# Block-sparse attention with a softplus feed-forward: the products with V of a set's two units at one place

## The chip, the cores and the metric

The kernel runs on one core of one Trainium2 chip. The metric is the device time of one execution in microseconds (us), lower is better. Three runs of the kernel before took 807.98, 808.40 and 809.11 us; their median is 808.4 us.

## The reference

Attention over 4 batches and 8 heads, 768 positions, head size 64. Positions form 24 blocks of 32. A query block sees its own block and the two neighbours, the first and the last block, and three sampled blocks; the first and the last query block see everything. The result is the input of a feed-forward layer with a softplus between two matrix products.

```python
scores = scale * np.matmul(q, k.transpose(0, 1, 3, 2))
mask = np.abs(blk_i - blk_j) <= window
mask = mask | (blk_i == 0) | (blk_j == 0) | (blk_i == n_blocks - 1) | (blk_j == n_blocks - 1)
...
scores = np.where(mask, scores, -1000000000.0)
scores = scores - np.max(scores, axis=-1, keepdims=True)
attn = np.exp(scores)
attn = attn / (np.sum(attn, axis=-1, keepdims=True) + 1e-09)
out = np.matmul(attn, v)
x = out.transpose(0, 2, 1, 3).reshape(B * S, H * D)      # 3072 x 512
h = x @ w_in                                             # 3072 x 2048
g = np.maximum(h, 0.0) + np.log1p(np.exp(-np.abs(h)))
return g @ w_out                                         # 3072 x 512
```

All is computed in fp32: the attention with fp32 matmuls, the feed-forward with operands that are split into a high and a low part (three matmuls for one).

## The kernel before

**Sets and units.** Queries are taken in groups of four query blocks (128 rows), six groups to a batch. Each group is a *set*, numbered in order; the sixth group of a batch has only two query blocks left (a half set) and is preceded by a *whole* set, which holds the rows of the first and last query block that see all keys. That makes 28 sets: per batch five full ones, one whole, one half. A set works on four pairs of heads and is cut into two *units*: `a = 0` is the first two pairs of heads, `a = 1` the other two (`NA` is 2). So there are 56 units, `units[n] = (m, a)`.

**What a unit does**, in this order:

- `scores` (L581): the products of queries and gathered keys into two PSUM tiles (tag `s`; matmuls of L601, of L625 in a whole set), then on VectorE the scaling, the mask and the row minimum `nmax` (L607, or L632 and L638).
- `exponents` (L642): ScalarE's exponential of four pieces, L657, with row sums.
- `transposes` (L661): eight TensorE transposes (L670, twelve in a whole unit) into two or three PSUM tiles of tag `s`, each copied to an SBUF tile `pt` (four buffers) by ScalarE (L677) or VectorE (L675). In a unit `a = 1` that isn't whole both copies are ScalarE's.
- `values` (L682): the products of `pt` with the gathered V, `vg`, into the PSUM tile `x` (L700, 64 profiled matmuls in a unit of a full set, 32 in a half set; L714 in a whole set). The tile `x` has one buffer; it is made at the unit `a = 0` and holds both units.

When a set's second unit is done, `normalise` (L721, VectorE, L728 to L730) divides by the sums and frees `x`, `turn` (L738) transposes the result on TensorE (L745), `x_high` (L757, ScalarE, L759) and `x_low` (L761, VectorE, L763) split it for the feed-forward.

**Pieces.** `pieces(n)` (L768) gives three pieces for place `n`: the score piece (`x_low` of a set that ended two places ago, `scores(n + 2)`), the value piece (`exponents(n + 2)`, `turn` of a set that ended one place ago, `values(n)`, and behind a set's second unit `load_values` of the set after next into the same one of two `vg` buffers), and the transpose piece (`x_high`, `normalise` of a set that ends here, `transposes(n + 1)`). `attend` (L862) runs the next piece, one gather of V and of keys (GpSimd, L567 and L511), and a tick of the conversion of the feed-forward's weights (`convert`).

**Order.** The first 22 pieces run by themselves (L885). After that the pieces are strewn into the feed-forward's first phase by `due` (L888): one step `j` of the feed-forward is `hidden(j)` (12 matmuls, L237 to L239, a piece may stand in the middle), and `project(j - 3)` (9 matmuls, L295 to L297, a piece may stand after each third of it). In the steady stretch a step takes one unit: the score piece in the middle of `hidden`, the value piece after the first third of `project`, the transpose piece behind `project`. The second phase of the feed-forward has no pieces. SyncE's queue runs in the program's order; on the other engines a planner places the instructions, by the program's order where they are ready in its own reckoning. The four PSUM buffers of tag `s` are shared by `scores`, `transposes`, `turn` and `hidden`, so each of those waits for an earlier one to be read out.

Of the kernel before, what the change touches and what calls it, by code (L numbers as in the profile page):

```python
# [50 lines left out]
def sparse_attention_ffn(  # L51
# [27 lines left out]
    NA = NP // 2  # L79
# [385 lines left out]
    def gathered(work, m):  # L465
        while work and work[0][0] <= m:
            work.pop(0)[1]()
# [50 lines left out]
    sets = []  # L518
# [58 lines left out]
    units = [(m, a) for m in range(len(sets)) for a in range(NA)]  # L577
# [103 lines left out]

    def values(n):  # L682
        m, a = units[n]
        b, g, whole = sets[m]
        pt = state[n]["pt"]
        gathered(value_work, m)
        vd = vg[sets[m]]
        if a == 0:
            xps[m] = ps_x.tile([P, DM], F32, tag="x", name=f"x{n}")
        xq = xps[m]  # L690

        if not whole:
            ni = NI if g < NG - 1 else 2
            for j in range(2):
                for r in range(2):
                    h = 2 * (2 * a + j) + r
                    for c in range(2):
                        for i in range(ni):
                            rows = slice(i * BLOCK, (i + 1) * BLOCK)
                            nc.tensor.matmul(  # L700
                                xq[rows, h * D : (h + 1) * D],
                                pt[r, 2 * j + c][:, rows],
                                vd[:, c, i, h * D : (h + 1) * D],
                                start=(c == 0), stop=(c == 1),
                            )
        else:
            rows_v = vd.rearrange("p c i f -> p (c i) f")
            for r in range(2):
                at = (2 * a + r) * D
                for c in range(NCH):  # L710
                    for o in range(2):
                        rows = slice(64 * o, 64 * o + 64)
                        h = 2 * (2 * a + o) + r
                        nc.tensor.matmul(  # L714
                            xq[rows, at : at + D],
                            pt[r, c][:, rows],
                            rows_v[:, c, h * D : (h + 1) * D],
                            start=(c == 0), stop=(c == NCH - 1),
                        )
# [48 lines left out]
    def pieces(n):  # L768
# [24 lines left out]
        def value_piece():  # L793
            if n + 2 < len(units):
                exponents(n + 2)
            if ended[1] is not None:
                turn(ended[1])
            if n < len(units):
                values(n)
                if ended[2] is not None:  # L800
                    load_values(ended[2] + 2)
            if scored is not None:
                load_queries(scored + 2)
# [177 lines left out]
```

## Time and profile before

| | us |
|---|---|
| median of the runs | 808.4 |
| span of the profiled execution | 812.1 |
| TensorE matmuls busy (PE) | 781.7 |
| VectorE busy (DVE) | 574.8 |
| ScalarE busy (ACT) | 489.6 |
| GpSimd busy (POOL) | 223.3 |

The span is that of one execution under the profiler, from the first to the last instruction; it is 3.7 us longer than the median of the runs. Busy time is the union of an engine's instructions. Matmuls are pipelined and their ends are modelled, so a busy PE isn't PE at its peak. PEld is the loading of matmul weights, which overlaps PE. In rows of the profile a name such as `x<-vg,pt` is the tile written and the tiles read, and `[3.19 <-ACT pt L677]` is idle time of the engine ahead of the instruction with what ended it; "issue" is idle time in which the engine waited for nothing that the profile shows.

### The profile page before, as it was taken

How to read it: one execution, taken by the hardware profiler on the slowest of the kernel's cores; microseconds unless marked ns; L12 is line 12 of the kernel's file. 1: busy time of each engine (PE TensorE's matmuls, PEld its weight loads, DVE VectorE, ACT ScalarE, POOL GpSimd, SP SyncE). 2: the span in 40 equal slices, each digit the busy share in tenths (PEclk: the TensorE clock that was granted, in tenths of full speed). 3: DMA queues.
4: the chain of work that ended last, by engine and by line, in shares of the span. 5: the costliest groups of instructions: out<-in, count | busy, mean ns of one | idle time of the engine just before them, and what ended most of it. 6: DMA issues, size and time to landing. Idle time of an engine off the chain costs nothing.

```text
span 812.1 us, 21433 instructions
## 1 busy us (share of the span) xinstructions
PE 781.7 (96%) x8108; PEld 647.6 (80%) x8108; DVE 574.8 (71%) x1474; ACT 489.6 (60%) x1182; POOL 223.3 (27%) x389
## 2 busy tenths in 40 slices
PE   8878898999999999999999999999999999999997
PEld 8545676877677777778778988999988999988996
DVE  5778999876887777886655985656565656656564
ACT  5878785757767767767565764444444444444442
POOL 6864775635565436563000000000000000000000
PEclk9999898999999999999999999999999999999999
DMA  8899678687696777866425640304040312122021
GB/s 254 241 257 336 171 212 266 195 294 247 184 291 198 248 261 200 267 171 184 158 78 182 250 178 20 137 1 155 2 146 10 116 40 105 52 88 68 0 79 40
DMA packets 48408, 129.65 MB, mean 160 GB/s; under 512 B 5489, under 2 KB 5617, under 8 KB 46257
## 3 DMA queue, kind: packets, MB, share of 16 engines
q1 hardware_dynamic: 42304, 109.79, 42.3%
q0 software_dynamic: 5712, 17.57, 7.6%
q8 instruction: 64, 1.05, 0.5%
q10 hardware_dynamic: 288, 0.93, 0.3%
q14 instruction: 40, 0.32, 0.1%
HBM read 97.85 MB, written 30.41 MB: 158 GB/s over the span
## 4 chain that ended last, share of the span: by engine, by line
PE 82%; DVE 7%; ACT 6%; DMA 2%; issue 2%; POOL 0%; SPq 0%; ACTq 0%; DVEq 0%; POOLq 0%
PE o L295 11%; PE h L237 11%; PE o L297 10%; PE o L296 10%; PE h L238 10%; PE h L239 10%; PE s L601 5%; PE t L670 4%; PE x L700 4%; ACT pr L657 3%; PE warm L831 2%; DMA kT<-in_k_dram 1%; PE s L625 1%; DVE pr L607 1%; PE x L714 1%
## 5 line engine op out<-in xcount | busy, mean ns | idle before, releaser
L237 PE MATMUL h<-x,w 128*128 128x384 f32 x512 | 180.0, 352 | 0.4 <-DVE nmax L632 0.2
L238 PE MATMUL h<-x,w 128*128 128x384 f32 x512 | 173.7, 339 | 0.0
L239 PE MATMUL h<-x,w 128*128 128x384 f32 x512 | 173.1, 338 | 0.0
L250 DVE TENSOR_SCALAR u<-e 128x384 f32<-128x384 f32 x128 | 50.8, 397 | 155.8 <-ACT e L244 154.4
L295 PE MATMUL o<-w,gh 128*128 128x512 f32 x384 | 158.7, 413 | 0.0
L657 ACT ACTIVATE pr<-pr,nmax 128x256 f32<-128x256 f32 (+2 forms) x208 | 110.4, 532 | 74.6 <-DVE nmax L607 60.4
L297 PE MATMUL o<-w,gl 128*128 128x512 f32 x384 | 152.0, 396 | 1.2 <-issue 1.0
L296 PE MATMUL o<-w,gh 128*128 128x512 f32 x384 | 151.7, 395 | 0.0
L243 ACT ACTIVATE e<-h 128x384 f32<-128x384 f32 x128 | 62.4, 487 | 114.9 <-PE h L239 114.8
L267 ACT CAST gh<-u 128x384 fp32r<-128x384 f32 x128 | 65.6, 513 | 79.2 <-PE o L296 78.1
L237 PEld LDWEIGHTS h<-x,w 128*128 128x128 f32 x512 | 96.6, 189 | 19.4 <-issue 11.2
L567 POOL DMA_INDIRECT vg<-in_v_dram,ix x88 | 90.3, 1027 | 65.9 <-PE x L700 39.1
L238 PEld LDWEIGHTS h<-x,w 128*128 128x128 f32 x512 | 96.8, 189 | 6.5 <-issue 2.2
L511 POOL COPY kg<-kT 128x128 f32 x252 | 86.0, 389 | 41.2 <-PE s L601 38.8
L239 PEld LDWEIGHTS h<-x,w 128*128 128x128 f32 x512 | 96.6, 189 | 0.0
L295 PEld LDWEIGHTS o<-w,gh 128*128 128x128 f32 x384 | 72.0, 188 | 19.9 <-issue 7.1
L297 PEld LDWEIGHTS o<-w,gl 128*128 128x128 f32 x384 | 72.1, 188 | 18.8 <-issue 1.5
L296 PEld LDWEIGHTS o<-w,gh 128*128 128x128 f32 x384 | 72.2, 188 | 10.3 <-issue 0.4
L607 DVE CUSTOM_DVE_ANT_1 pr<-s,mask 128x256 f32<-128x256 f32 (+1 forms) x192 | 69.6, 414 | 14.5 <-PE s L601 14.5
L258 ACT ACTIVATE u<-u 128x384 f32<-128x384 f32 x128 | 66.9, 523 | 15.4 <-DVE e L252 15.2
L263 DVE TENSOR_TENSOR u<-u,e 128x384 f32<-128x384 f32 x128 | 73.6, 575 | 3.0 <-ACT u L258 2.4
L273 DVE TENSOR_TENSOR gl<-u,gh 128x384 fp32r<-128x384 f32 x128 | 73.0, 570 | 2.8 <-ACT gh L267 2.8
(81 smaller groups left out, 1088.6 us busy)
## 6 DMA issues: line engine op xcount, KB each, us to landing
vg<-in_v_dram SPq DMA_DIRECT2D x19, 768.0 KB, 5.8
xD<-x SPq DMA_DIRECT2D x8, 1536.0 KB, 7.4
x<-xD SPq DMA_DIRECT2D x8, 1536.0 KB
raw<-in_w_in_dram SPq DMA_DIRECT2D x16, 512.0 KB, 9.3
raw<-in_w_out_dram SPq DMA_DIRECT2D x16, 512.0 KB, 8.3
qc<-in_q_dram SPq DMA_DIRECT2D x24, 256.0 KB, 6.9
vg<-in_v_dram SPq DMA_DIRECT2D x12, 512.0 KB, 7.4
yD<-os SPq DMA_DIRECT2D x24, 256.0 KB, 2.5
```

The source lines that it names most:

```text
L237: nc.tensor.matmul(ph, wh[:, cols], hi[:, c], start=(c == 0), stop=False)
L238: nc.tensor.matmul(ph, wh[:, cols], lo[:, c], start=False, stop=False)
L239: nc.tensor.matmul(ph, wl[:, cols], hi[:, c], start=False, stop=(c == NC - 1))
L263: nc.vector.tensor_tensor(out=l, in0=l, in1=e, op=ALU.add)
L273: nc.vector.tensor_tensor(out=gl, in0=l, in1=G[n].bitcast(F32), op=ALU.subtract)
L295: nc.tensor.matmul(po[m], gh[:, cols], wh, start=first, stop=False)
L296: nc.tensor.matmul(po[m], gh[:, cols], wl, start=False, stop=False)
L297: nc.tensor.matmul(po[m], gl[:, cols], wh, start=False, stop=last)
L511: copy(out=kd[:, i, 1 + NR + s, :], in_=kT[b][:, bass.ds(x, 1), :].rearrange("p n f -> p (n f)"))
L567: nc.gpsimd.indirect_dma_start(out=vd[0 : 3 * BLOCK, 1, i, :], out_offset=None, in_=v, in_offset=bass.IndirectOffsetOnAxis(ap=ix[:, b, 4 * ...
L607: nc.vector.tensor_tensor_reduce(out=pr[r][rows, j], in0=ps[r][rows, j], in1=mask[rows, g].unsqueeze(2).to_broadcast([ni * BLOCK, NS, BLOCK]),
L657: nc.scalar.activation(x, x, AF.Exp, bias=nmax[rows, r, j : j + 1], scale=-1.0, accum_out=rs[rows, h : h + 1])
```

## The change

The body of `values` becomes `products`, and the new `values` decides when it is called. For a set that isn't whole, nothing is multiplied at the unit `a = 0`; at the unit `a = 1` the products of both units are made, the first unit's first. In a whole set each unit's products stay where they were.

```diff
     def values(n):
         m, a = units[n]
+        whole = sets[m][2]
+        if a == NA - 1 and not whole:
+            for n_ in range(n - NA + 1, n + 1):
+                products(n_)
+        elif whole:
+            products(n)
+
+    def products(n):
+        m, a = units[n]
         b, g, whole = sets[m]
         pt = state[n]["pt"]
         gathered(value_work, m)
```

The value piece still runs `exponents(n + 2)`, `turn`, `values(n)` and `load_values` in this order, and there are still three pieces to a unit.

## The prediction, made before the changed kernel was run

> **What bounds the kernel now.** I read the page first: busy times, the granted clock, the chain that ended last.
>
> ```profile
> span 812.1 us, 21433 instructions
> PE 781.7 (96%) x8108; PEld 647.6 (80%) x8108; DVE 574.8 (71%) x1474; ACT 489.6 (60%) x1182; POOL 223.3 (27%) x389
> PEclk9999898999999999999999999999999999999999
> PE 82%; DVE 7%; ACT 6%; DMA 2%; issue 2%; POOL 0%; SPq 0%; ACTq 0%; DVEq 0%; POOLq 0%
> ```
>
> TensorE is busy 96% of the span and carries 82% of the chain. The change takes no matmul away, so it can only act on the 30.4 us in which PE is idle (812.1 - 781.7), on the clock, or by making new idle time. Next I cut the span in three windows; the columns are length, then busy us and instructions of PE, PEld, DVE, ACT, POOL, the granted clock, DMA share and GB/s.
>
> ```profile
> 0.00:140.00 140.00, 118.52 (x1942) 88.25 (x1943) 116.32 (x341) 101.92 (x264) 95.13 (x168) 0.94 0.86 252
> 140.00:432.00 292.00, 287.27 (x4295) 221.26 (x4294) 219.65 (x646) 202.50 (x541) 128.17 (x221) 1.00 0.68 207
> 432.00:812.00 380.00, 375.94 (x1875) 338.12 (x1873) 238.81 (x489) 185.19 (x378) 0.00 (x0) 1.00 0.25 89
> ```
>
> The last window has no attention and doesn't change. In the first, PE is idle 21.5 us and DVE is nearly as busy as PE. In the middle, the steady stretch, PE is idle 4.7 us of 292: PE bounds it, and a delay of PE there is paid in full. The waits of PE in that stretch, longest first (total, times, longest):
>
> ```profile
> PE t L670 <- DVE x L763: 1.8, 1, 1.8
> PE s L601 <- ACT pt L677: 1.2, 2, 1.0
> PE o L297 <- issue: 1.0, 1, 1.0
> ```
>
> None of them is a wait of the products themselves. So the change removes no wait here; the question is what it brings.
>
> **The change part by part.** *Removed and added instructions:* none. A unit's products issue only TensorE work, no DMA and nothing on SP, POOL, ACT or DVE, and the gathers that `products` would force are long popped by the pieces between. *Moved:* the first unit's 64 products go behind one transpose piece, one score piece and the feed-forward's matmuls between, to the second unit's place. One step of the steady stretch shows it (start, duration):
>
> ```profile
> 151.43 0.60 PE L745 MATMUL y<-ident,xs 128*128 128x128 f32 x4
> 151.96 1.10 PE L700 MATMUL x<-vg,pt 128*32 128x64 f32 x64
> 152.99 0.50 PE L295 MATMUL o<-w,gh 128*128 128x512 f32 x1
> ...
> 154.49 1.03 PE L670 MATMUL t<-ident,pr 128*128 128x128 f32 x8
> ...
> 156.51 1.09 PE L601 MATMUL s<-kg,qc 64*32 64x256 f32 x32
> ...
> 159.49 1.10 PE L700 MATMUL x<-vg,pt 128*32 128x64 f32 x64
> ```
>
> The products at 151.96 hold PE for 152.99 - 151.96 = 1.03 us. After the change everything from 152.99 to 159.49 comes 1.03 us earlier on PE, and when the group at 159.49 ends, PE has done the same work as before. The end of a set's products, and so `normalise`, the release of `x` and of the V buffer, stays where it was if nothing between waits. The group of `turn` stays at the first unit's place, so PE changes tile shapes as often as before: nothing. The `pt` tiles of the first unit live a unit longer, all four buffers are then full, but the next copies into them follow transposes that stand behind the products on PE anyway: nothing.
>
> *Term 1, the scores come before their PSUM is free.* The score piece between the two units needs PSUM that ScalarE's copies of the transposes release. ScalarE in the same step (idle before in brackets):
>
> ```profile
> 150.60 0.51 ACT L657 ACTIVATE pr<-pr,nmax 128x256 f32<-128x256 f32 x1 [2.13 <-DVE nmax L607]
> ...
> 155.79 1.07 ACT L677 COPY pt<-t 128x512 f32<-128x512 f32 x2
> 156.75 0.53 ACT L267 CAST gh<-u 128x384 fp32r<-128x384 f32 x1
> ```
>
> From 150.60 to 156.75 ScalarE has no idle row: exponentials, the feed-forward's part, and last the two copies, of which the first ends near 155.79 + 1.07 / 2 = 156.3. That run begins with scores made before 151.96, so the change doesn't move it. The scores start at 156.51, about 0.2 us after the first copy. Taken 1.03 us earlier, PE would wait some 0.8 us here, and reach the end of the merged products 0.8 us late. Two half sets wait already, which are the 1.2 us of the list above; one of them:
>
> ```profile
> 326.03 1.36 PE L601 MATMUL s<-kg,qc 64*32 64x256 f32 x32 [0.95 <-ACT pt L677]
> ```
>
> Behind the waiting scores on PE stand the feed-forward's matmuls and the merged products; DVE waits for the scores, ScalarE for both. The delay doesn't come once a set. When PE is 1.03 us late, it meets the next set's ScalarE run as late as it does now, unless that run is late too, which it is only where it starts right at its scores (in the step above ScalarE had waited 2.13 us for `nmax`). And idle time that stands now takes lateness back: the 0.95 us above, and 1.82 us here, set by V-independent work:
>
> ```profile
> 203.82 0.44 PE L670 MATMUL t<-ident,pr 128*128 128x128 f32 x2 [1.82 <-DVE x L763]
> ```
>
> I take one full 1.03 us and two thirds of a second one, 1.7 us. Ends: nothing, if the planner fills the wait; 4.1 us, one full delay in each of four batches.
>
> *Term 2, instruction blocks.* PE's idle time named "issue" falls at a fixed distance:
>
> ```profile
> 41.41:49.84 8.44, 5.30 (x127) 3.39 (x126) 5.50 (x17) 5.85 (x15) 7.47 (x17) 1.00 1.05 274
> 49.84:61.45 11.61, 9.91 (x253) 6.74 (x253) 10.10 (x36) 9.57 (x28) 6.20 (x7) 1.00 0.87 247
> 61.45:261.88 200.43, 187.45 (x2785) 141.15 (x2785) 169.07 (x459) 145.91 (x386) 115.05 (x186) 0.97 0.79 241
> ```
>
> ```profile
> 49.85 0.64 PE L601 MATMUL s<-kg,qc 64*32 64x256 f32 x8 [2.11 <-issue]
> 61.46 0.76 PE L700 MATMUL x<-vg,pt 128*32 128x64 f32 x37 [0.39 <-issue]
> 261.89 0.50 PE L297 MATMUL o<-w,gl 128*128 128x512 f32 x1 [1.02 <-issue]
> ```
>
> ```profile
> q8 instruction: 64, 1.05, 0.5%
> ```
>
> Between these stalls lie 253, 506 and 5570 matmuls and weight loads: 1, 2 and 22 times 253, and the instruction queue brought 64 packets for 16216 of them, 253 each. So PE's instructions come in blocks, and PE stalls when the next block's packet is behind data (DMA share 0.79 to 1.05). Two merged units are 64 x 2 x 2 = 256 such instructions in 2.06 us, a whole block, where a steady set now spreads two blocks over 16 us:
>
> ```profile
> 251.13:267.93 16.79, 15.77 (x255) 12.27 (x254) 11.99 (x31) 11.43 (x31) 8.96 (x16) 1.00 0.66 206
> 261.88:267.93 6.04, 6.03 (x59) 4.61 (x59) 3.70 (x10) 3.03 (x7) 1.47 (x5) 1.00 0.45 163
> ```
>
> From the boundary at 261.89 to the second unit's products at 267.93 are 118 instructions; with 128 of the first unit put there, that boundary falls about ten behind the start of the merged run, and the next about ten behind its end. A set is 509, two blocks within 1%, so this holds for the four full sets from 228 to 285 us; in the other batches the boundary falls in the run's middle, where both blocks last as long as now. In those four sets the next block must be there within about 3 us. Shown stalls are 0.39 to 2.11 us; I take two of 1.5 us and take off the 1.02 us that stands there now: 2.0 us. Ends: -1.0 us, and four stalls of 2.11 us less 1.02, 7.4 us.
>
> The Trainium skill, "Runtime: NRT & Kernel Launch", section "Instruction fetch mechanics", says that instructions are refilled in blocks of 256 while the current one runs, and that crossing a boundary is mostly hidden. The trace agrees with the block and not with "hidden" at the four boundaries that stall. By that page the sum would lack this term.
>
> *Term 3, the start.* Waits that the moved products touch there:
>
> ```profile
> 27.88 0.65 PE L700 MATMUL x<-vg,pt 128*32 128x64 f32 x16 [3.19 <-ACT pt L677]
> 43.92 0.30 PE L700 MATMUL x<-vg,pt 128*32 128x64 f32 x2 [0.48 <-DMA vg<-in_v_dram,ix]
> 44.75 0.97 PE L700 MATMUL x<-vg,pt 128*32 128x64 f32 x50 [0.53 <-DMA vg<-in_v_dram,ix]
> 50.53 0.42 DVE L607 CUSTOM_DVE_ANT_1 pr<-s,mask 128x256 f32<-128x256 f32 x1 [3.31 <-PE s L601]
> 51.06 0.51 ACT L657 ACTIVATE pr<-pr,nmax 128x256 f32<-128x256 f32 x1 [3.02 <-DVE nmax L607]
> 20.00:40.00 20.00, 16.07 (x424) 11.45 (x426) 14.42 (x53) 17.25 (x49) 16.73 (x37) 0.91 0.86 240
> ```
>
> The V wait of 0.48 + 0.53 us goes, since those products come a unit later. The block stall at 49.85 now stands inside scores, and DVE and ScalarE wait 3 us for them; with the products behind those scores it stands inside products. But PE meets the next boundary at 61.46, late already, after as many instructions as before, so what DVE and ScalarE win they wait away there. I take 0. Ends: -3.3 us, DVE's whole wait, and +1.0 us, one unit's products on the path.
>
> *Sum:* 0 + 1.7 + 2.0 = 3.7 us. On the profiled span that is 812.1 + 3.7 = 815.8 us; that execution stands 3.7 us over the median, and the difference goes on the median: 808.4 + 3.7 = 812.1, said as **812.0 us**.
>
> **The rivals.**
>
> *The start is won.* Moving the products behind the scores of the second unit frees DVE and ScalarE up to 3.3 us earlier at 50.53, and the products of set 0's first unit shorten the idle 3.19 us before 27.88. This decides if PE is past the boundary at 61.46 earlier than now and the steady terms stay under it. Time: 808.4 - 3.3 + 0.7, one small wait left, = 805.8 us. For it: DVE is the busy engine up to 140 us, so time that it wins may last. Against it: the boundary. The clock speaks for it: 0.91 in the window of 20 to 40 us is 20 x 0.09 = 1.8 us of lost clock. The Trainium skill, "TensorE: Matmul & The Clock Gate", Part 1, puts such a loss down to an idle window of about 3.4 us; the 3.19 us and the window's clock agree, and by that rule alone, with the products in the gap, the estimate would be 1.8 us less than without it.
>
> *Blocks stay hidden.* Term 2 is 0 because the packets come in time, and the 1.02 us stays: 808.4 + 1.7 = 810.1 us. For it: only four of 64 boundaries stall now.
>
> *Nothing moves.* The planner, which orders PE's work by readiness, puts the first unit's products into places where its reckoning has PE idle, or ScalarE's run follows PE after all: 808.4 us. Against it: in the step above the order on PE is the program's.
>
> **How the numbers follow.** Chances: forecast (812.0) 0.42, blocks hidden 0.16, nothing moves 0.20, the start won 0.22. A measurement of this kernel tells 0.2%, 1.6 us, from no change. The start won gives faster 0.22. Nothing moves gives same, and so does half of blocks hidden, since 810.1 lies on the bound of 810.0: 0.20 + 0.08 = 0.28. Slower is the rest, 0.42 + 0.08 = 0.50. The low end is 805.0 us, term 3 at its end with nothing else (805.1). At the upper end terms 1 and 2 at their ends, 4.1 + 7.4, would give 819.9; both at once is left out, and one at its end with the other as taken, 1.7 + 7.4, gives 817.5 us. The forecast's own range is 810.1 to 817.5.
>
> **What would show it.** Right: in 140 to 432 us PE waits for `pt` L677 at scores between a set's units more than twice, and "issue" rows stand at or just behind products at 228 to 285 us; the last window keeps its 380 us. Wrong: term 1, if scores at those places start without a wait though the products before them are gone; term 2, if no issue row stands there; term 3, if the scores that end at 50.4 us now end near 45 and everything up to 140 us stays earlier. An order on PE with the first unit's products at their old places would make all of it void.

## The result and the profile after

The change makes the kernel **slower**: 819.46 us is the median after (818.51, 818.90, 820.02 and 1238.37 us), 808.75 us that of the kernel before beside it. The ratio is 1.0114 (95% interval 1.0083 to 1.0144), 7 to 12 us; executions that ran slow at a lower granted clock, such as that of 1238.37 us (0.56), count in no ratio of this document. Two later groups of runs gave 1.0126 (1.0081 to 1.0171) and 1.0144 (1.0118 to 1.0170). The forecast was 812.0 with an upper end of 817.5: the sign was right, the size a third of what came, and the time lies outside the range.

The page after, the lines that answer to those shown of before:

```profile
span 816.4 us, 21433 instructions
PE 781.4 (96%) x8108; PEld 646.8 (79%) x8108; DVE 579.7 (71%) x1474; ACT 488.2 (60%) x1182; POOL 226.3 (28%) x389
...
PE 70%; DVE 12%; ACT 10%; DMA 5%; issue 3%; SPq 0%; DVEq 0%; ACTq 0%
```

TensorE's work is the same, 781.4 us; the span is 4.3 us longer and all of that is idle time of PE. The pair of profiles shows less than half of the loss: 816.4 us is the span of the run that took 818.51, 2.1 us less than its time, so a run of before with the median's 808.4 us would have a span near 806.3. Its profiled execution of 812.1 us was a late one. So below, stretches of several traces are compared, and medians.

The same three windows of the trace after, with the columns as in the prediction:

```profile
0.00:140.00 140.00, 118.64 (x1880) 85.96 (x1880) 115.78 (x342) 102.20 (x267) 97.75 (x168) 0.96 0.86 252
140.00:432.00 292.00, 282.61 (x4285) 218.81 (x4286) 222.01 (x639) 199.53 (x536) 128.54 (x221) 0.99 0.68 207
432.00:812.00 380.00, 380.00 (x1949) 342.00 (x1945) 241.05 (x493) 186.44 (x381) 0.00 (x0) 1.00 0.25 87
```

In the steady stretch PE is idle 9.4 us (292.00 - 282.61) instead of 4.7. What it waits for there, in the list of waits:

```profile
PE t L670 <- issue: 2.5, 1, 2.5
PE o L297 <- issue: 1.8, 1, 1.8
...
PE s L601 <- ACT pt L677: 0.4, 1, 0.4
```

Two "issue" waits lead the list, 4.3 us where before had 1.0. The wait of the scores for ScalarE's copies, which the prediction expected more of, has fallen from 1.2 to 0.4 us. The timeline of PE shows where the first two stand:

```profile
235.03 1.99 PE L709 MATMUL x<-vg,pt 128*32 128x64 f32 x128
...
240.20 0.39 PE L297 MATMUL o<-w,gl 128*128 128x512 f32 x1 [1.81 <-issue]
...
283.05 1.99 PE L709 MATMUL x<-vg,pt 128*32 128x64 f32 x128
...
288.48 1.18 PE L670 MATMUL t<-ident,pr 128*128 128x128 f32 x8 [2.55 <-issue]
```

These are the merged runs of sets 14 and 17: 128 matmuls and as many weight loads in 1.99 us, and a few instructions later PE stands still. Those of sets 15 and 16, between, have no such row. Behind the longer stall the granted clock falls, as the window with the stall and the one behind it show (the last but two numbers are clock, DMA share, GB/s):

```profile
282.80:289.36 6.56, 4.01 (x142) 3.20 (x140) 4.08 (x16) 3.58 (x12) 1.83 (x2) 1.00 0.96 303
289.36:292.77 3.41, 3.41 (x11) 2.70 (x9) 2.69 (x5) 1.49 (x3) 0.00 (x0) 0.50 1.05 276
```

3.41 us at half clock are another 1.7 us. The stalls lie whole blocks apart, as before: between them, in windows from one to the next,

```profile
64.40:240.19 175.79, 162.21 (x2406) 120.97 (x2407) 149.33 (x407) 127.36 (x333) 103.31 (x166) 0.98 0.79 242
240.19:288.47 48.28, 45.61 (x760) 36.34 (x759) 38.91 (x107) 33.15 (x92) 24.43 (x35) 1.00 0.79 236
```

are 4813 and 1519 matmuls and weight loads, 19.02 and 6.00 times 253.

The trace also holds the times of the single packets of the instruction queue (q8 in the prediction), though no view lists them one by one. The packet before the end of the first stall runs from 237.69 to 238.77 us, the one before the end of the second from 286.28 to 287.22; PE goes on 1.43 and 1.26 us after they have landed. In sets 15 and 16 the packet had landed at 252.80 and 267.47 us, at the latest 0.5 us into the run (which starts at 252.32 and 267.49). The two late packets took 1.09 and 0.93 us, no longer than the median of all 64, 1.12. What was late is their start, and what held that up is not shown: the prediction's "behind data" stays an argument.

### The profile page after: what moved, and what is told of

Its sections match the earlier page's. It is cut to its first block, busy times and chain, and to the rows that moved or that the text cites. A ratio compares the mean times of both kernels' runs of the same rounds, so it can differ in the third digit from the quotient of the medians.

```text
span 816.4 us, 21433 instructions
## 1 busy us (share of the span) xinstructions
PE 781.4 (96%) x8108; PEld 646.8 (79%) x8108; DVE 579.7 (71%) x1474; ACT 488.2 (60%) x1182; POOL 226.3 (28%) x389
## 4 chain that ended last, share of the span: by engine, by line
PE 70%; DVE 12%; ACT 10%; DMA 5%; issue 3%; SPq 0%; DVEq 0%; ACTq 0%
PE h L237 10%; PE o L295 10%; PE h L238 9%; PE h L239 9%; PE o L297 9%; PE o L296 9%; ACT pr L657 4%; PE x L709 4%; PE s L601 3%; PE t L670 3%; DMA vg<-in_v_dram 2%; DVE pr L607 2%; PE s L625 1%; DVE wt L178 1%; DVE kg L497 1%
## 5 line engine op out<-in xcount | busy, mean ns | idle before, releaser
L250 DVE TENSOR_SCALAR u<-e 128x384 f32<-128x384 f32 x128 | 46.1, 360 | 151.8 <-ACT e L244 151.8
L511 POOL COPY kg<-kT 128x128 f32 x252 | 91.2, 408 | 48.6 <-PE s L601 46.5
L273 DVE TENSOR_TENSOR gl<-u,gh 128x384 fp32r<-128x384 f32 x128 | 72.9, 569 | 7.9 <-ACT gh L267 7.9
L263 DVE TENSOR_TENSOR u<-u,e 128x384 f32<-128x384 f32 x128 | 77.8, 608 | 1.0 <-ACT u L258 0.4
L252 DVE SCALAR_TENSOR_TENSOR e<-u,e 128x384 f32<-128x384 f32 x128 | 72.5, 567 | 3.8
```

The costliest lines, as they stand in the source:

```text
L263: nc.vector.tensor_tensor(out=l, in0=l, in1=e, op=ALU.add)
L273: nc.vector.tensor_tensor(out=gl, in0=l, in1=G[n].bitcast(F32), op=ALU.subtract)
L511: copy(out=kd[:, i, 1 + NR + s, :], in_=kT[b][:, bass.ds(x, 1), :].rearrange("p n f -> p (n f)"))
```

## The experiments

Each kernel below is the change with one edit; each got five rounds beside the kernel before on the same chip. There were two kinds of chip: on one the kernel before takes 808 to 810 us (the result above, and the group with the shift), on the other 831 to 834 us (the other groups). Ratios are to the kernel before of the same group. Most edits only choose the sets `m` that are merged, with another condition in this place of `values`:

```diff
-        if a == NA - 1 and not whole:
+        if whole or not (CONDITION):
+            products(n)
+        elif a == NA - 1:
             for n_ in range(n - NA + 1, n + 1):
                 products(n_)
-        elif whole:
-            products(n)
```

### Which sets cost: start, steady stretch, sets 14 to 17

The kernel before, as it stands (no edit), for the noise of the group:

> The kernel before once more, timed against itself, for a second profile of it. The profile of before spans 812.1 us, that of after 816.4 us: 4.3 us apart, where the medians are 10.7 us apart. Theory A (the profile of before is of an execution that lost some 5 us by chance): ratio 1.000 within 0.002, and a span near 806 us, with the 5 us missing at clock-gated stretches or block stalls of the first 140 us. Theory B (the profiler costs before more than after): a span near 812 us again.

Measured: 1.0007 (0.9979 to 1.0034). The span of its trace, 831.0 us, stands 2.2 us under the 833.16 us of that execution, much as after the change (2.1), so theory B gets no support. Theory A's span of 806 us can't be read from it, since this chip takes 834 us for the kernel.

`m < 6`, the start alone:

> Only sets 0 to 4 merge their two units' products; from set 6 on each unit has its own place. Theory block and PSUM in the steady stretch (terms 1 and 2): most of the loss is in the steady stretch, so this costs 0 to 3 us over before. Theory start (the first 140 us pay): 6 to 10 us over before.

Measured: 1.0032 (1.0012 to 1.0052), 2.7 us.

`m >= 6`, the steady stretch alone:

> Only sets from 6 on merge; sets 0 to 4 are as before. Theory terms 1 and 2: 7 to 10 us over before. Theory start: 0 to 4 us over before. If the losses add, this and the start-only kernel sum to 10.7 us.

Measured: 1.0086 (1.0055 to 1.0117), 7.2 us. Two rows of its PE timeline, behind the runs of sets 14 and 17:

```profile
251.66 1.09 PE L670 MATMUL t<-ident,pr 128*128 128x128 f32 x8 [2.00 <-issue]
...
305.70 1.49 PE L670 MATMUL t<-ident,pr 128*128 128x128 f32 x8 [2.39 <-issue]
```

`not 14 <= m <= 17`, all but four sets:

> All sets merge but 14 to 17, the four in which a merged run fills an instruction block from end to end. Theory block stalls (term 2): the issue rows at 240 and 288 us go, with the half clock after the second, and it costs 4 to 6 us less than after. Theory PSUM (term 1) alone: four of 24 sets less, 1 to 2 us less than after.

Measured: 1.0040 (1.0013 to 1.0067), 3.3 us.

So start and steady stretch add: 0.32% + 0.86% = 1.18%, where the change costs 1.14 to 1.44%. And four sets of 24 carry most of it on this kind of chip: without them 0.40% are left. That fits the blocks. It doesn't prove them, since sets 14 to 17 might be dear for another reason.

### Shifting the instruction stream by half a block

The change again, and sets 14 to 17 alone (`14 <= m <= 17`):

> The changed kernel again, on the chip of the runs beside it. Both theories: 1.008 to 1.015 times the kernel before, 7 to 13 us. Block theory: issue rows just behind the merged runs of sets 14 to 17 (some 230 to 305 us), on two to four of the four sets, 1.5 to 2.6 us each, and a stretch of half clock behind one of the longer ones. PSUM theory: no such rows are needed, PE loses its time in waits for VectorE's and ScalarE's read-outs in every batch.

> Only sets 14 to 17 are merged, 4 of the 24 sets that the change merges. Block theory: most of the steady loss is here, 4 to 7 us over before (1.005 to 1.008), with issue rows behind these four runs. PSUM theory: a sixth of the sets, so about a sixth of the change's loss, 1 to 2 us (1.001 to 1.002).

Measured: 1.0126 (1.0081 to 1.0171) and 1.0042 (1.0020 to 1.0065), 3.4 us. The second lies between the ranges of the two theories. Then both the kernel before and the change with 128 more instructions on TensorE ahead of all sets:

```diff
-WARM = 50
+WARM = 46
...
         nc.tensor.matmul(warm[:, n % 4], ident, ident, start=True, stop=True)
+    for n in range(36):
+        nc.tensor.matmul(warm[0:32, n % 4, 0:64], ident[:, 0:32], ident[:, 0:64], start=True, stop=True)
```

> The kernel before with TensorE's instruction stream shifted by 128 instructions: four of the warm-up's 50 matmuls go (16 instructions) and 36 small matmuls of the products' shape come behind them (144). Output unchanged. Both theories: within 3 us of before (0.997 to 1.003), since no run of this kernel is as long as a block.

> The change with the same shift of 128 instructions. Block theory: the boundaries fall in the middle of the merged runs of sets 14 to 17 (offset about 135 of 256 instead of 6 to 12), so no issue row stands behind them; now the runs of sets 7 to 10 and 21 to 24 (some 145 to 200 and 345 to 400 us) have them at their ends, where the DMA share is 0.69 and 0.70 instead of 0.85, so stalls there are shorter or none. Time over c3: 2 to 8 us, with the rows at the new places. PSUM theory: loss and places as in c1, 7 to 13 us over c3, issue rows or not.

Measured: 1.0066 (1.0038 to 1.0093) and 1.0157 (1.0125 to 1.0188). The first is a miss of both theories: the shift alone costs 5.3 us. The trace shows more stalls in the start. PE's timeline of the shifted kernel before:

```profile
29.40 1.93 PE L601 MATMUL s<-kg,qc 64*32 64x256 f32 x25 [3.05 <-issue]
...
41.97 0.98 PE L700 MATMUL x<-vg,pt 128*32 128x64 f32 x49 [1.42 <-issue]
...
52.77 0.32 PE L700 MATMUL x<-vg,pt 128*32 128x64 f32 x8 [0.82 <-issue]
...
61.69 1.09 PE L601 MATMUL s<-kg,qc 64*32 64x256 f32 x31 [2.33 <-issue]
```

These are 7.6 us of stalls up to 70 us, where before had 3.4. No run of a whole block is needed there; the DMA share is 0.90 from 20 to 70 us. (The traced execution took 811.75 us, 2.6 less than the median of this kernel, so it doesn't show all of the 5.3 us.)

What the pair was for is in the steady stretch. One window per kernel, from the first matmul of the feed-forward's step 16 to that of step 24, which holds sets 14 to 17; before, its shifted version, sets 14 to 17 alone, the change, the change shifted:

```profile
220.90:286.84 65.94, 64.78 (x1058) 51.17 (x1057) 52.02 (x154) 47.63 (x133) 36.33 (x62) 1.00 0.79 247
```

```profile
217.46:282.34 64.88, 64.88 (x1057) 51.58 (x1056) 51.97 (x154) 47.61 (x133) 36.63 (x62) 1.00 0.81 251
```

```profile
215.08:285.55 70.47, 65.68 (x1057) 52.09 (x1056) 55.63 (x156) 47.88 (x134) 37.00 (x62) 0.98 0.80 245
```

```profile
220.98:290.74 69.76, 65.28 (x1079) 52.08 (x1072) 56.77 (x158) 47.98 (x135) 37.40 (x63) 0.99 0.83 250
```

```profile
226.36:291.25 64.89, 64.41 (x1079) 51.74 (x1072) 54.58 (x155) 46.79 (x133) 37.30 (x63) 1.00 0.81 252
```

Split, the stretch takes 65.94 and 64.88 us. Merged it takes 70.47 and 69.76. Merged and shifted it takes 64.89, as if nothing were merged: the same sets, the same order, the same early scores, only the block boundaries elsewhere. The stalls moved to where the shift put them, behind the runs of sets 7, 10, 21 and 24. PE's timeline of the shifted change:

```profile
134.55 0.80 PE L297 MATMUL o<-w,gl 128*128 128x512 f32 x1 [3.76 <-issue]
...
184.49 0.39 PE L297 MATMUL o<-w,gl 128*128 128x512 f32 x1 [1.19 <-issue]
...
286.93 1.99 PE L709 MATMUL x<-vg,pt 128*32 128x64 f32 x128
...
289.65 1.03 PE L670 MATMUL t<-ident,pr 128*128 128x128 f32 x8
...
353.44 1.09 PE L670 MATMUL t<-ident,pr 128*128 128x128 f32 x8 [2.11 <-issue]
...
399.87 1.03 PE L670 MATMUL t<-ident,pr 128*128 128x128 f32 x8 [1.10 <-issue]
```

Set 17's run (286.93) goes on without a gap. The other traces agree. In all six with sets 14 to 17 merged and their boundaries not shifted, PE stalls behind the runs of sets 14 and 17, not behind those of 15 and 16, for 1.81 to 2.67 us, and each of the twelve stalls ends 1.24 to 1.51 us after an instruction packet has landed; the four shifted ones above end 1.25 to 1.72 us after one. The stretch itself takes 69.15 us in the second trace of the change. On the other kind of chip it takes 74.62 to 76.71 us in the three traces with these sets merged and not shifted, and 68.27 to 69.49 in the eight without.

This settles the blocks as the cause of the loss in sets 14 to 17. In all the shift gains nothing, since two other batches pay instead: the change with the shift stands 1.0157 / 1.0066 = 1.009 over the kernel before with it. By the medians these are 8.0 us; they lie at the end of the block theory's 2 to 8 and inside the PSUM theory's 7 to 13; the places of the stalls tell the two apart, the time doesn't.

### Set 7, the later sets, and a shift for one batch

The merged traces show another place: a wait of transposes and one of `hidden` some 11 and 14 us behind the start of set 7's merged run, at the transposes of set 8's second unit. In the second trace of the change, PE and then VectorE:

```profile
138.58 1.32 PE L670 MATMUL t<-ident,pr 128*128 128x128 f32 x8 [2.15 <-DVE nmax L607]
141.63 0.69 PE L237 MATMUL h<-x,w 128*128 128x384 f32 x1 [1.74 <-DVE e L253]
```

```profile
133.91 2.30 DVE L263 TENSOR_TENSOR u<-u,e 128x384 f32<-128x384 f32 x1
...
136.94 0.16 DVE L737 TENSOR_SCALAR sums<-sums 128x8 f32<-128x8 f32 x1
137.05 0.69 DVE L178 SCALAR_TENSOR_TENSOR wt<-raw,wt 128x512 int32<-128x512 int32 x1
137.66 0.42 DVE L607 CUSTOM_DVE_ANT_1 pr<-s,mask 128x256 f32<-128x256 f32 x1
```

And the same place where set 7 isn't merged (sets 14 to 17 alone):

```profile
131.39 0.41 DVE L607 CUSTOM_DVE_ANT_1 pr<-s,mask 128x256 f32<-128x256 f32 x1
...
132.77 1.06 DVE L178 SCALAR_TENSOR_TENSOR wt<-raw,wt 128x512 int32<-128x512 int32 x1
133.75 0.16 DVE L737 TENSOR_SCALAR sums<-sums 128x8 f32<-128x8 f32 x1
```

The row minima are those of set 9's first scores. With the merge the planner puts the sums' step of set 8 and a conversion of weights (L178) ahead of them, and `u` takes 2.30 us there. Until they have read the scores, two of the four PSUM tiles are held, and the transposes need one; PE, which has no products of set 8's first unit to do there, meets that wait in full. So this is term 1's mechanism, with VectorE in ScalarE's place (the expectation below puts it down to late exponentials, wrongly: the transposes' own are long done).

Such a wait isn't the merge's alone, though. The kernel before has one in both of its traces, a unit earlier, at the transposes of set 8's first unit: 2.79 us in the trace of the prediction, behind a long step of VectorE, and 2.76 us in its second trace. PE and VectorE before:

```profile
127.69 1.09 PE L670 MATMUL t<-ident,pr 128*128 128x128 f32 x4 [2.79 <-DVE nmax L607]
```

```profile
121.03 4.80 DVE L250 TENSOR_SCALAR u<-e 128x384 f32<-128x384 f32 x1 [0.85 <-ACT e L244]
```

What the wait behind set 7 costs in the end was asked with `m == 7`, and what the rest of the sets costs with `m > 7 and not 14 <= m <= 17`:

> Only set 7 is merged, the first full set of the second batch. Order theory (the planner puts the sums' step and a conversion of weights ahead of the second unit's row minima on VectorE, so ScalarE's exponentials and the transposes come late, and TensorE's idle time halves its clock): 3 to 6 us over before (1.004 to 1.007), with a wait of the transposes for nmax of some 2.1 us and one of hidden for e of 1.5 to 1.7 us near 130 to 145 us, and half clock behind them. Block theory alone: within 1 us of before, since the boundary falls in the middle of this run.

> All sets from 8 on are merged but 14 to 17: the steady stretch without the two places. Block and order theories: within 2 us of before (0.998 to 1.002), no issue row behind a merged run. PSUM theory (scores wait for ScalarE's copies in every batch): 1.5 to 4 us over.

Measured: 1.0006 (0.9991 to 1.0022) and 1.0008 (0.9985 to 1.0030). The order theory fails in its price: in the trace of `m == 7` both waits stand there, the first shorter,

```profile
144.68 1.32 PE L670 MATMUL t<-ident,pr 128*128 128x128 f32 x8 [0.78 <-DVE nmax L607]
147.73 0.44 PE L237 MATMUL h<-x,w 128*128 128x384 f32 x1 [1.74 <-DVE e L253]
```

and the time is that of before. (It may cost more where the first wait is 2.1 us; that stays open.)

The later sets cost nothing measurable in sum, but the traces show a loss and a gain in it. Steps 4 to 8 of the feed-forward hold the runs of sets 7 and 8, steps 32 to 36 those of sets 23 and 24. In the trace of the second kernel above they take 41.40 and 36.10 us, in that of the kernel before on the same kind of chip 39.70 and 38.81. On the first kind they take 41.87 and 32.23 us after the change, 37.13 and 33.44 with only sets 14 to 17 merged. So a measured sum of nothing doesn't show that early scores cost nothing anywhere.

The last of this group leaves the start alone and moves the boundaries of sets 14 to 17 only; beside it the change:

```diff
+            twice = 2 if m in (13, 20) else 1
             for j in range(2):
-                for r in range(2):
+                for r in list(range(2)) * twice:
```

> The change, but the products of sets 13 and 20 are made twice, with the same result: 128 more instructions and 1.03 us more work of TensorE at each of the two. That moves the boundaries of sets 14 to 17, and of no other full set, by half a block, into the middle of their runs. Block theory: no issue row behind them, and in spite of 2.1 us more work 1.5 to 5 us less than the change alone on this chip. PSUM theory and order theory alone: 2 us more than the change alone.

> The change again, beside the three on one chip: 1.009 to 1.015 times before, by all theories, with the issue rows behind sets 14 and 17 and the two waits near 135 us.

Measured: 1.0127 (1.0083 to 1.0170) and 1.0144 (1.0118 to 1.0170). In the trace with the doubled products no "issue" row stands on PE between 55 and 440 us; the stalls of sets 14 to 17 are gone once more. But steps 16 to 24 take 74.44 us in that execution, one of the longest of its kernel at 850.80 us, against 74.62 in the trace of the change beside it: `hidden` waits 4.0 us for `e` there (2.9 in the other), and a spell of half clock stands from 288.40 to 291.81 us. So this trace shows where the stalls went and no gain of time. The times don't show one either: 0.17% less with 2.1 us (0.25%) more work would be 3.5 us gained, but the intervals are 0.5 to 0.9% wide. (The boundaries of set 18, a full set as well, moved too, against the expectation's words; no stall stands there in either trace.)

### Do the parts add, and what is the rest?

`not 14 <= m <= 17`, `m < 6`, `m > 0 and not 14 <= m <= 17`, and `14 <= m <= 17`, on one chip:

> All sets that the change merges but 14 to 17, beside their complement. If the two parts add: 1.004 to 1.008 over before, 3 to 6.5 us, so that this and the run of sets 14 to 17 alone give the change's 1.011 to 1.014 together. If the parts only cost together (each hides what the other loses): below 1.003 here and below 1.004 there.

> Only sets 0 to 4 are merged. Start theory: nearly all that sets other than 14 to 17 cost, 2 to 5 us over (1.0025 to 1.006), as much as the run without 14 to 17. Set 7 theory (its 3 to 4 us late transposes last on this chip): within 0.2% of before here, and the run without 14 to 17 3 us above it.

> As the run without 14 to 17, but set 0 isn't merged either. If the start's loss is set 0's, whose end came 4 to 7 us late in each merged trace: within 0.2% of before, 2 to 4 us under the run without 14 to 17. If it comes from sets 1 to 4 or 7: the same as that run, 1.003 to 1.007.

> Only sets 14 to 17 are merged. Block theory: one or two issue rows of 1.8 to 2.7 us behind these runs and 4.4 us more from the 16th to the 24th step of the feed-forward, 1.004 to 1.0075 over before. If the loss there needed the other merged sets: below 1.003.

Measured: 1.0037 (1.0006 to 1.0069), 1.0007 (0.9980 to 1.0034), 1.0003 (0.9969 to 1.0036) and 1.0076 (1.0045 to 1.0107). The parts add: 0.37% + 0.76% = 1.13%. Sets 14 to 17 alone cost 6.3 us here, again with two stalls:

```profile
242.63 1.52 PE L670 MATMUL t<-ident,pr 128*128 128x128 f32 x8 [1.87 <-issue]
...
297.58 1.72 PE L670 MATMUL t<-ident,pr 128*128 128x128 f32 x8 [2.56 <-issue]
```

The rest, 3 us, could not be split. Without set 0 it is 0.03%, as the theory of set 0 has it; the start alone, which holds set 0, gave 0.32% once and 0.07% now, and the second is what the theory of set 7 has. Both can't be right alone, and all these intervals overlap. What the traces show of set 0 is its end, `x_low`, first before, then after the change:

```profile
34.52 0.67 DVE L763 TENSOR_TENSOR x<-y,x 128x512 fp32r<-128x512 f32 x1
```

```profile
39.57 0.69 DVE L772 TENSOR_TENSOR x<-y,x 128x512 fp32r<-128x512 f32 x1
```

It comes 5.1 us later. How much of that reaches the end of the program stays open.

On the first kind of chip, that of the forecast, the rest is the larger part: sets 14 to 17 alone cost 0.42% and the change 1.26%, so 0.84%, 6.8 us, would lie elsewhere. The run without these sets was made only on the other kind, but the traces place that part. Step 16, where the stretch of sets 14 to 17 begins, starts at 215.08 us with only these sets merged (that execution took 812.49 us, its kernel's median is 812.43), at 220.98 in the change's first trace and at 224.98 in its second. That is 5.9 and 9.9 us later, and these executions took 6.0 and 8.6 us longer in all. So in these traces the rest of the loss stands ahead of set 14. In both traces of the change 4.8 and 4.2 us of it come in steps 4 to 8; the instruction stalls up to 70 us are 6.4 us in both, twice the 3.2 us of the trace with only sets 14 to 17 merged. These are single executions, and no experiment on this kind of chip takes one of the places away: which mechanism costs how much there stays open.

## Why the prediction was right in sign and too small

- **Removed and added instructions: none; the last window unchanged.** Right: 781.4 us of matmuls, and the window from 432 us on shows no new wait.
- **Term 2, the blocks: place and mechanism right, size too small.** "In the other batches the boundary falls in the run's middle" and "for the four full sets from 228 to 285 us" held to the set, and in fact two of the four stalled, as taken. But they were taken at 1.5 us each, inside the range of the stalls before, 0.39 to 2.11, none of which stood behind a block as short as these; they measured 1.81 and 2.55 us here, and 1.82 to 2.67 in the other traces. And the half clock behind them, 1.7 us in the trace of the change, was left out of the term, though the prediction had named that rule for the start. Taken 2.0 us; measured 3.4 us (0.42%) on the first kind of chip, 6.3 us (0.76%) on the second, where this is the step that failed most. The term's upper end, 7.4, held it. That two of four would stall was a guess that came true: what holds a packet up isn't shown, so nothing here says why it was sets 14 and 17.
- **Term 1, early scores behind ScalarE's copies: wrong.** Taken 1.7 us; the wait fell from 1.2 to 0.4 us where more than two such waits were called the sign of being right, and merging all sets from 8 on but 14 to 17 costs 0.08% (-0.15 to 0.30). The mechanism was looked for on the wrong engine: where PE did come too early, behind set 7, it waited for tiles that VectorE held, in an order that the planner had changed, and merging set 7 alone cost 0.06% (-0.09 to 0.22).
- **Term 3, the start: taken as 0 with an upper end of 1.0. On the first kind of chip this is the step that failed most.** There the two traces of the change are 5.9 and 9.9 us late by set 14, against the one with only sets 14 to 17 merged. On the other kind all sets but 14 to 17 cost 0.40% and 0.37% in two groups, 3 us, and the later ones 0.08%, so by the middle values most of it lies ahead of set 14 there too, though the intervals would allow otherwise. The V wait did go. But the term let a block stall move from the scores into the products for nothing, and took the boundary at 61.46 us to be met as late as before: the stall there now ends at 64.41 us, and at 63.51 in the second trace. Set 0 ends 5 us later, and the block stalls of the start grow from 3.4 to 6.4 us, three of them inside merged products, by the waits of PE up to 140 us after the change:

```profile
PE x L709 <- issue: 5.1, 3, 1.9
```

  And the waits on VectorE in steps 4 to 8, behind set 7, stand in no term. How the loss splits over sets 0 to 13 is open.
- **The range.** It left out both terms at their ends at once, and gave the start 1.0 us at most. With 3.4 us for the blocks and the 6.8 that are left on the first kind of chip, 808.4 grows to 818.6, close to the 819.46 measured; the 6.8 is a difference of two runs there, not a run of its own.
- **The rivals.** "The start is won" is refuted in sign; "blocks hidden" by the rows; "nothing moves" too, since the steady order on PE was the program's (each merged run in one piece).

## What to carry to other kernels

Count instructions, not only microseconds: a stretch that issues a whole block of them (253 in these traces) in about 2 us can leave the next block no time to arrive. Here two of four such runs stalled, for 1.8 to 2.7 us, some with a spell of half clock behind. The DMA share was 0.79 to 0.83 in these stretches; no run tried it with idle DMA. Gathering small matmuls in one place can therefore cost what spreading them among long ones hid. Where such a stall shows, look for the instruction packet that lands just before its end, shift the stream by half a block and see whether the stall moves; but look at the start again, since a shift moves its stalls too. And a part that costs nothing in sum can hide a loss in one place and a gain in another, which the times of single steps show.

## What the runs showed of the hardware that was not expected

**Half clock comes by the place of a stall, not its length alone.** In the trace with sets 14 to 17 merged, a stall of 1.99 us (ends at 234.17) is followed by half clock, and one of 2.67 us (ends at 283.98) isn't:

```profile
231.56:234.97 3.41, 1.42 (x10) 0.98 (x9) 3.31 (x8) 1.10 (x4) 2.70 (x4) 1.00 0.94 274
234.97:238.38 3.41, 3.41 (x33) 2.54 (x39) 0.84 (x2) 1.06 (x2) 3.02 (x3) 0.50 1.06 286
...
279.33:282.75 3.42, 1.98 (x83) 1.55 (x72) 1.98 (x8) 2.67 (x9) 1.71 (x2) 1.00 0.84 247
282.75:286.16 3.41, 2.18 (x15) 2.04 (x15) 2.01 (x4) 1.54 (x3) 0.13 (x1) 1.00 1.02 348
```

The windows are cut where the clock can change: in each trace its changes lie a whole number of 3.413 us apart (in this one the spell before ends at 95.02, 41 such lengths ahead of 234.97). The shorter stall falls into one window and leaves PE busy for 1.42 us of it; the longer is cut in two by the boundary at 282.75, and PE is busy for 1.98 and 2.18 us. In the change's trace, windows with 0.88 and 1.61 us are followed by half and by full clock. The busy time isn't a sharp threshold: over all traces some windows with more of it are followed by half clock.

The Trainium skill, "TensorE: Matmul & The Clock Gate", Part 1, gives a free-running window of about 3.4 us for it. The length of the spell, 3.41 us, agrees; that an idle window is needed doesn't, since 1.99 us of idle time sufficed.

**A step of VectorE can take several times as long beside GpSimd.** In the page after, the 128 steps of this kind take 608 ns on average:

```profile
L263 DVE TENSOR_TENSOR u<-u,e 128x384 f32<-128x384 f32 x128 | 77.8, 608 | 1.0 <-ACT u L258 0.4
```

The one of 2.30 us at 133.91, in the second trace of the change, ends behind this row of GpSimd:

```profile
134.46 1.32 POOL L182 TENSOR_TENSOR wt<-wt,raw 128x512 int32<-128x512 int32 x1
```

The Trainium skill, "SBUF — State Buffer", Terms, says that the two share a port pair and that the loser waits for the whole instruction. The two rows agree with it. So do the others: in all 18 traces, 105 steps of VectorE in the feed-forward's softplus (L250, L252, L253, L263, L273) took over 2.5 times their line's median, among them the 4.80 us above, and each overlaps a step of L182 on GpSimd; of the 11415 others 295 do. No run took GpSimd's step away, so the cause isn't shown.

**The same kernel takes 810 us on one chip and 831 to 834 on others.** The stretch of sets 14 to 17 takes 65.94 us on the first; on the second the kernel before has

```profile
228.38:297.21 68.83, 66.11 (x1058) 51.74 (x1057) 52.08 (x154) 47.57 (x133) 36.39 (x62) 1.00 0.75 234
```

with 234 GB/s instead of 247. The change's ratio was alike on both, the part of sets 14 to 17 was not (0.42 and 0.76%). What sets the chips apart isn't shown.
